# Fewer loads in the prologue, work in the lead-in, a side job on more slots, and a later normalization in an attention kernel on one Trainium2 core

## The chip, the cores and the metric

The kernel runs on one core of a Trainium2 chip. The core has TensorE (PE, matrix products; its weight loads are listed as PEld), VectorE (DVE), ScalarE (ACT), GpSimd (POOL) and SyncE (SP), whose queue issues all the transfers of this kernel. The metric is the device time of one execution in microseconds; a kernel's time is the median of several runs.

## The reference, cut to what matters

Two branches are computed on 2048 tokens of width 640 and mixed with a gate per token. Branch A is attention with 32 heads of 20 columns over four segments of 512 tokens, with a memory matrix per head that is read before and written after each segment. Branch B routes one token (the highest score) through a feed-forward layer and leaves all other tokens as they are.

```python
for s in range(N):                       # N = 4 segments of L = 512
    qs, ks, vs = q[:, :, s], k[:, :, s], v[:, :, s]
    p = softmax(einsum("bhqd,bhkd->bhqk", qs, ks) * scale + mask)
    a_dot = einsum("bhqk,bhkd->bhqd", p, vs)
    a_mem = einsum(phi(qs), M) / (einsum(phi(qs), z) + 1e-6)
    outs.append(g * a_mem + (1 - g) * a_dot)      # g: a gate per head
    M = M + einsum(phi(ks), vs); z = z + phi(ks).sum()
a = concat(outs) @ wo
...
idx = argsort(-(x @ w_r))[:1]            # the one routed token
y = (silu(x[idx] @ w_gate) * (x[idx] @ w_up)) @ w_down * sigmoid(r[idx])
b = x, with y added to row idx
return G * a + (1 - G) * b               # G = sigmoid((x * gate_w).sum(-1))
```

## The kernel before

The work is cut into 8 units (2 halves of the heads, 4 segments each) and 32 groups of 4 heads, four to a unit. Matrices are kept as a high and a low part, so each product of the projections is three matmuls.

**Projections.** For each unit nine jobs are computed in the order T0, T1, T2, V0, V1, T3, V2, T4, V3: a T job gives 128 columns of queries and keys for 512 tokens (15 matmuls of 512 columns), a V job gives the values of 128 tokens (15 matmuls of 320 columns, 322 in the first half, with two extra columns `rg` for the router and the gate). `load_t`, `load_v` and `load_x` bring raw weights and inputs into a ring of four buffers named `raw`; `split_t`, `split_v`, `split_x` make the two parts on ScalarE and VectorE or GpSimd (tiles `whi`, `wlo`, `xhi`, `xlo`). `prefetch(u, job)` says at which job each load and split is written. After a T job `evac_t` splits the result (`hi`, `lo`) and `place` writes it to DRAM (`stkq`, `stkk`); `bring_back` reads it from there as `qs` and `ks`, six matmuls into the next job, in the layout that the logits need. At that point the variable `groups[0]` also tells which groups have been placed. Small steps wait in a list `tail` and are taken at fixed points of the next job: `keys` (transposes `ktp`), `memory_read` (products `nm`), `memory_write` (products `mp`).

**Attention.** The main loop goes over groups n = -2 to 31, six slots each. `a_step` computes logits (`a`) of a group that comes later, from which VectorE takes row maxima (`junk`, `mx`); `m_split` and `m_rows` turn the maxima into two extra rows of `qs` (`mneg`, the transpose `mtp`, the copy `mr`, four small transfers `qs<-mr`), needed by `b_step` of that group at its slot 0. `b_step` computes the logits with the maxima subtracted (`bt`), ScalarE the exponentials (`p`), GpSimd the causal mask; `pv_step` multiplies with the values (`va`), in two halves, at slot 5 of the group and slot 1 of the next one. `norm` (transposes `otp`, then `rs`, `rs`, `ou` on VectorE) and `store` (`otok`) follow.

**What fills the time.** `fill(at)` runs projection matmuls until the projections are 3.7 groups ahead; it is called twice in each slot from group -1 on. In group -2 and before `a_step` the projections only run as far as `groups[0]` asks.

**The side job.** Routing and the feed-forward layer are a generator `ffn` whose steps end at each `yield 1`. It is started at slot 0 of group 13 and advanced by one step at each `pv_phase`, twice per group. `route` has 12 steps, each with a small transfer or a small operation: row maxima to DRAM (`rrow`), back as a row (`row`), its maximum (`top`), to DRAM (`sel`), back to all partitions (`all`), and this twice. `ffn_up` takes 10 steps (5 for the gate, 5 for the up matrix; each brings two weight tiles `wt` of 442 KB and multiplies those of the step before), `ffn_act` works on ScalarE, VectorE and GpSimd (`fe`) and goes through DRAM (`hrow`, `ht`), `ffn_down` takes 8 steps, and `yrow`, `yb`, `y` end it. At slot 0 of group 28 what is left of it is run at once (`f.finish()`), and then the last stage starts, `out_stage`: for each of 16 tiles of 128 tokens it loads `otok` (`ot`), transposes (`ttp`), splits (`oh`, `ol`), multiplies with `wo` (`acc` of line 721) and mixes.

**What sets the order.** TensorE and SP execute in the order in which the code is written. On the other engines a scheduler chooses a fixed order when the program is built. Small results of TensorE (`acc`, `ktp`, `nm`, `mp`, `mtp`, `otp`, `ffn`, `ttp`) share three PSUM buffers (`misc`).

Of the kernel before, what the change touches and what calls it, by code (L numbers as in the profile page):

```python
# [20 lines left out]
HH = H // NH  # L21
# [34 lines left out]
def tile_infini_mod(  # L56
# [100 lines left out]
    def w_tile(key):  # L157
        w, tag, bufs = (VC + 2, "wv", KT) if key[0] == "V" else (D, "w", KT + 1)
        hi = pool.tile([128, w], F32R, tag=tag + "hi", bufs=bufs, name="whi")
        lo = pool.tile([128, w], F32R, tag=tag + "lo", bufs=bufs, name="wlo")  # L160
        W[key] = hi, lo
        return hi, lo
# [21 lines left out]

    def load_w(key):
        if key[0] == "V":
            r = slice(128 * key[2], 128 * key[2] + 128)
            srcs = [columns("v", key[1], g, 2 * GC)[r] for g in (0, 2)]
            if key[1] == 0:
                srcs.append(wc[r, WQ:WQ + 2])  # L190
            raw_tile(key, *srcs)
        else:
            raw_tile(key, wo[128 * key[1]:128 * key[1] + 128, :])

    def split_w(key, eng=None):
        raw = raws.pop(key)
        hi, lo = w_tile(key)
        split(hi[:, :raw.shape[1]], lo[:, :raw.shape[1]], raw, eng or nc.gpsimd)
# [104 lines left out]
    def evac_v(u, c, acc):  # L303
        hf, s = divmod(u, SEG)
        nc.scalar.copy(sub(va[u % 2], c * (HH * VW + 11), [[VW, HH], [1, DH]]),
                       acc[:, :VC].rearrange("p (h d) -> p h d", d=DH))
        if hf == 0:
            nc.vector.tensor_copy(rg[:, :, 4 * s + c], acc[:, VC:VC + 2])
# [9 lines left out]
    def prefetch(u, job):  # L318

        hf, s = divmod(u, SEG)  # L320
        if u == 0:
            if job == "T0":
                load_t(0, 1)
                split_t(0, 1, nc.vector)
                load_t(0, 2)
            elif job == "T1":
                split_t(0, 2, nc.vector)
            elif job == "T2":
                split_v(0, (0, 1, 2, 3), nc.vector)
                load_v(0, (4,))  # L330
                load_t(0, 3)
            elif job == "V0":
                split_v(0, (4,), nc.vector)
                split_t(0, 3)
                load_t(0, 4)
            elif job == "V1":
                split_t(0, 4)
        if u == SEG:
            if job == "T0":
                load_v(1, (0, 1, 2, 3))  # L340
            elif job == "T1":
                split_v(1, (0, 1, 2, 3))
                load_v(1, (4,))
            elif job == "T2":
                split_v(1, (4,))
# [17 lines left out]

    def load_v(hf, ks_):
        for k in ks_:
            load_w(("V", hf, k))

    def split_v(hf, ks_, eng=None):
        for k in ks_:
# [501 lines left out]
```

## Time and profile before

| | |
|---|---|
| median of 3 runs | 762.35 us (755.8 to 767.57) |
| the profiled execution | 758.56 us |
| its span, first to last instruction | 756.6 us |
| TensorE busy | 662.8 us (88%) |
| VectorE, ScalarE, GpSimd busy | 428.1, 356.8, 213.9 us |
| granted TensorE clock, mean over the span | 0.935 of full speed |

The profiled execution lies 0.5% below the median. The span is shorter than the execution by 2.0 us, which lies around the instructions. A granted clock of 1.0 is 2.4 GHz, and one of 0.5 is 1.2 GHz.

### The profile page before, as it was taken

The page shows a single profiled execution, that of the slowest core. Times are in us where ns is not written, and L with a number is a line of the kernel's source. Part 1 is how long each engine was busy: PE and PEld are TensorE (multiplying, and loading weights), DVE is VectorE, ACT ScalarE, POOL GpSimd, SP SyncE. Part 2 cuts the span into 40 slices and gives each one's busy share as a digit, 9 for nine tenths or more (in the row PEclk, how much of TensorE's full clock was granted, in tenths as well). Part 3 has the DMA queues.
Part 4 walks back from the last instruction along what each step waited for, and adds up shares of the span by engine and source line. Part 5 has one row for each costly group of instructions (what it writes and reads, how often), then busy time and mean ns, then how long its engine had stood idle before and what let it go on. Part 6 is the DMA issues. An engine that isn't in the chain of part 4 may idle for free.

```text
span 756.6 us, 13400 instructions
## 1 busy us (share of the span) xinstructions
PE 662.8 (88%) x4496; PEld 448.6 (59%) x4496; DVE 428.1 (57%) x1498; ACT 356.8 (47%) x608; POOL 213.9 (28%) x322
## 2 busy tenths in 40 slices
PE   4278989998997999899979998999889656999997
PEld 2256656665664666456656665655566216777787
DVE  7235556665666467656645666666657314664453
ACT  5313546555566466555634555545545202444421
POOL 4102313332344355423411332234434100111100
PEclk9669999999999899999968999999999755999999
DMA  5726653646465557565852576768565634334453
GB/s 161 190 53 177 177 144 96 169 126 165 113 179 151 153 141 186 142 141 151 152 138 69 159 223 208 221 192 254 146 186 166 176 113 151 114 116 133 145 168 105
DMA packets 82932, 116.31 MB, mean 154 GB/s; under 512 B 37734, under 2 KB 43376, under 8 KB 82864
## 3 DMA queue, kind: packets, MB, share of 16 engines
q1 hardware_dynamic: 82864, 115.46, 55.8%
q8 instruction: 36, 0.59, 0.4%
q14 instruction: 32, 0.26, 0.1%
HBM read 72.94 MB, written 41.96 MB: 152 GB/s over the span
## 4 chain that ended last, share of the span: by engine, by line
PE 67%; DMA 13%; DVE 6%; ACT 6%; issue 5%; SPq 3%; POOL 0%; POOLq 0%; ACTq 0%
PE acc L391 17%; PE acc L396 9%; PE pv L497 9%; PE bt L477 9%; PE acc L721 7%; PE a L446 6%; PE nm L272 3%; DVE junk L449 2%; DMA wt<-in_wd_dram 2%; DMA wt<-in_wu_dram 2%; DVE lo L247 2%; DMA raw<-in_wc_dram 2%; PE ktp L263 2%; PE otp L518 1%; ACT hi L246 1%
## 5 line engine op out<-in xcount | busy, mean ns | idle before, releaser
L449 DVE CUSTOM_DVE_ANT_0 junk<-a,mask 128x512 bf16<-128x512 f32 (+3 forms) x512 | 249.9, 488 | 132.8 <-PE a L446 123.0
L481 ACT ACTIVATE p<-bt 128x768 f32<-128x768 f32 (+1 forms) x192 | 169.6, 883 | 198.3 <-PE bt L477 190.2
L484 POOL TENSOR_SCALAR_AFFINE_SELECT p<-p 128x256 f32<-128x256 f32 (+1 forms) x192 | 94.7, 493 | 350.1 <-ACT p L481 350.0
L446 PE MATMUL a<-ks,qs 60*128 60x256 f32 (+2 forms) x512 | 81.5, 349 | 26.3 <-DMA ks<-stkk 13.5
L477 PE MATMUL bt<-qs,ks 62*128 62x256 f32 (+2 forms) x512 | 95.8, 407 | 7.2 <-ACT p L481 5.0
L391 PE MATMUL acc<-xhi,whi 128*128 128x512 f32 x200 | 86.8, 434 | 10.0 <-ACT xhi L149 7.7
L391 PE MATMUL acc<-xhi,wlo 128*128 128x512 f32 x200 | 91.1, 456 | 0.0
L391 PE MATMUL acc<-xlo,whi 128*128 128x512 f32 x200 | 87.5, 438 | 0.0
L497 PE MATMUL pv<-p,va 128*32 128x512 f32 (+3 forms) x1024 | 84.9, 451 | 0.0
L477 PEld LDWEIGHTS bt<-qs,ks 62*128 62x128 f32 x512 | 44.5, 189 | 62.1 <-issue 40.7
L446 PEld LDWEIGHTS a<-ks,qs 60*128 60x128 f32 x512 | 48.6, 193 | 37.3 <-DMA ks<-stkk 13.8
L391 PEld LDWEIGHTS acc<-xhi,whi 128*128 128x128 f32 x200 | 39.8, 199 | 30.0 <-issue 12.3
L396 PE MATMUL acc<-wlo,xhi 128*128 128x322 f32 (+1 forms) x160 | 55.3, 345 | 0.0
L721 PE MATMUL acc<-whi,oh 128*128 128x320 f32 x160 | 53.2, 332 | 1.7 <-DVE ol L689 1.5
L396 PE MATMUL acc<-whi,xhi 128*128 128x322 f32 (+1 forms) x160 | 54.2, 339 | 0.0
L150 POOL TENSOR_TENSOR xlo<-raw,xhi 128x512 fp32r<-128x512 f32 x37 | 47.3, 1290 | 19.3 <-ACT xhi L149 18.1
L391 PEld LDWEIGHTS acc<-xlo,whi 128*128 128x128 f32 x200 | 39.8, 199 | 20.8 <-issue 14.7
L396 PE MATMUL acc<-whi,xlo 128*128 128x322 f32 (+1 forms) x160 | 51.6, 322 | 0.0
L721 PE MATMUL acc<-whi,ol 128*128 128x320 f32 x160 | 51.5, 322 | 0.0
L721 PE MATMUL acc<-wlo,oh 128*128 128x320 f32 x160 | 50.3, 314 | 0.0
L497 PEld LDWEIGHTS pv<-p,va 128*32 128x32 f32 x1024 | 27.3, 111 | 37.7 <-issue 27.8
L391 PEld LDWEIGHTS acc<-xhi,wlo 128*128 128x128 f32 x200 | 40.3, 202 | 13.6 <-issue 9.7
(105 smaller groups left out, 932.8 us busy)
## 6 DMA issues: line engine op xcount, KB each, us to landing
qs<-stkq SPq DMA_DIRECT2D x64, 240.0 KB
ks<-stkk SPq DMA_DIRECT2D x64, 240.0 KB
raw<-in_xT_dram SPq DMA_DIRECT2D x40, 256.0 KB
stkq<-hi SPq DMA_DIRECT2D x32, 320.0 KB
stkq<-lo SPq DMA_DIRECT2D x32, 160.0 KB
otok<-ou SPq DMA_DIRECT2D x32, 160.0 KB
xf<-in_x_dram SPq DMA_DIRECT2D x16, 320.0 KB
out_dram<-xf SPq DMA_DIRECT2D x16, 320.0 KB
```

The source lines that it names most:

```text
L150: eng.tensor_tensor(out=lo, in0=raw, in1=f32(hi), op=OP.subtract)
L247: nc.vector.tensor_tensor(out=lo[:, :L], in0=acc, in1=f32(hi)[:, :L], op=OP.subtract)
L272: nc.tensor.matmul(nm[:, c, :], e[:GC, 128 * c:128 * c + 128], mbd[:, g, :], start=True, stop=True)
L391: nc.tensor.matmul(acc, a, b, start=i == 0, stop=i == 3 * KT - 1)
L396: nc.tensor.matmul(acc[:, :w], a, b, start=i == 0, stop=i == 3 * KT - 1)
L446: nc.tensor.matmul(a[:, b, at:at + nw], q_, k_, start=True, stop=True)
L449: nc.vector.tensor_tensor_reduce(out=junk[:, :w], in0=a[:, b, at:at + w], in1=mask[:, L - w:], scale=1.0, scalar=-3e38, op0=OP.add, op1=OP ...
L477: nc.tensor.matmul(bt[:, b, at:at + nw], k_, q_, start=True, stop=True)
L481: nc.scalar.activation(pt, bt[:, :, at:at + w], AF.Exp, scale=SCALE)
L484: nc.gpsimd.affine_select(out=d, in_=d, pattern=[[0, 2], [0, k], [1, 128]], base=0, channel_multiplier=-1, compare_op=OP.is_ge, fill=0.0)
L497: nc.tensor.matmul(pv[n][32 * j:32 * j + 32, L - w:], va[u % 2][:, c, VW * h:VW * h + 32], pt_tiles[n, j % 2, min(c, 2)][:, j // 2, at:at ...
L721: nc.tensor.matmul(acc[:, :n], a_[:, 128 * k:128 * k + 128], b_[:, n * b:n * b + n], start=i == 0, stop=i == 3 * KT - 1)
```

## The change

The value weights of a half come in four loads (`VPARTS`: 3 or 2 blocks of 128 rows, two column ranges) instead of ten or fifteen, into one wide tile; in the first unit they are issued before the placed results of T0, or right behind them, and the loads for T3 and T4 later than before. Before the loop the projections run up to 1.9 groups, group -2 begins at slot 3, and `fill` runs in it too. `groups[0]` is set at the twelfth matmul of a job, not the sixth, and `tail` steps are taken after matmuls 6, 9, 12 and 14, not 4, 7, 10 and 13. Steps of the side job that brought weights end with `yield 2` and are still advanced by `pv_phase`; all others are advanced at the end of every slot. `norm` moves from slot 2 to slot 4 and `store` from slot 3 to slot 5. In `out_stage` a tile whose rows were not loaded ahead waits three half-slots after its loads.

```diff
+    VPARTS = ((0, 0, 3), (0, 3, 5), (1, 0, 3), (1, 3, 5))
+    def load_v(hf, i):
+        qt, k0, k1 = VPARTS[i]
+        w = 2 * GC + (2 if hf == 0 and qt == 0 else 0)
...
+        nc.sync.dma_start(t, columns("v", hf, 2 * qt, w).rearrange("(k p) m -> p k m", p=128)[:, k0:k1])
...
             if job == "T0":
                 load_t(0, 1)
+                load_t(0, 2)
+                load_v(0, 0)
                 split_t(0, 1, nc.vector)
-                load_t(0, 2)
             elif job == "T1":
+                load_v(0, 1)
+                load_v(0, 2)
                 split_t(0, 2, nc.vector)
+                load_v(0, 3)
             elif job == "T2":
-                split_v(0, (0, 1, 2, 3), nc.vector)
-                load_v(0, (4,))
+                for i in range(4):
+                    split_v(0, i, nc.vector)
+            elif job == "V0":
                 load_t(0, 3)
...
                         if i == 6:
                             bring_back()
+                        if i == 12:
                             groups[0] = landed
-                            if (u, job) == (0, "T1"):
-                                load_v(0, (0, 1, 2, 3))
...
-                        if i in (4, 7, 10, 13):
+                        if i in (6, 9, 12, 14):
...
             wt = [ffn_load(rows[t, :, 2 * FC * hf:2 * FC * hf + 2 * FC], 2 * FC, 128) for hf in range(2)]
-            yield 1
+            yield 2
...
-            loads(t)
+            if t not in ot and t not in rows:
+                loads(t)
+                for _ in range(3):
+                    yield None
...
         for f in side:
-            f.run(1.0)
-
+            if f.last == 2:
+                f.debt = 0.0
+                f.run(1.0)
+
+    proj.until(lambda: chunks[0] >= 1.9)
     for n in range(-2, NG):
-        for slot in range(6):
+        for slot in range(0 if n > -2 else 3, 6):
...
-            if n >= -1:
-                fill(6 * n + slot)
+            fill(6 * n + slot)
...
-            if n >= 1 and slot == 2:
+            if n >= 1 and slot == 4:
                 done = norm(n - 1)
-            if n >= 1 and slot == 3:
+            if n >= 1 and slot == 5:
                 store(n - 1, done)
                 ready[0] = n - 1
+            for f in side:
+                if f.last != 2:
+                    f.debt = 0.0
+                    f.run(1.0)
```

On SP's queue in the lead-in, between the placed results of T0 and the first keys (`ks_107`), the program before has this, behind the last of twelve value loads (the first row):

```order
L144 DMA raw<-in_wc_dram 128x2
L224 DMA stkq_72<-hi 80x2x512
L226 DMA stkq_72<-lo 80x512
L224 DMA stkk_76<-hi 32x2x512
L226 DMA stkk_76<-lo 32x512
L224 DMA stkk_77<-hi 16x2x512
L226 DMA stkk_77<-lo 16x512
L144 DMA raw<-in_wc_dram 128x160 x2
L144 DMA raw<-in_wc_dram 128x2
L168 DMA raw<-in_wc_dram 128x5x80 x2
L239 DMA qs_109<-stkq_72 60x1024 x2
L239 DMA ks_107<-stkk_76 60x1024 x2
```

The changed program has this at the same place, behind the first of its four value loads:

```order
L192 DMA raw<-in_wc_dram 128x2x162
L192 DMA raw<-in_wc_dram 128x3x160
L192 DMA raw<-in_wc_dram 128x2x160
L250 DMA qs_106<-stkq_71 60x1024 x2
L235 DMA stkq_72<-hi 80x2x512
L237 DMA stkq_72<-lo 80x512
L235 DMA stkk_76<-hi 32x2x512
L237 DMA stkk_76<-lo 32x512
L235 DMA stkk_77<-hi 16x2x512
L237 DMA stkk_77<-lo 16x512
L250 DMA qs_109<-stkq_72 60x1024 x2
L250 DMA ks_107<-stkk_76 60x1024 x2
```

The value loads no longer stand between T0's queries and T1's results, and the loads for T3 (`128x5x80 x2`) no longer stand ahead of the first keys.

On SP's queue at slots 2 and 3 of group 14 of the changed program, the second pass of the routing (`all`, `rrow`, `row`) and the rows of maxima for group 15 (`qs_106<-mr`) stand like this:

```order
L572 DMA sel<-top_3429 1x1
L250 DMA ks_113<-stkk_78 60x1024 x2
L575 DMA all_3505<-sel 128x1
L560 DMA rrow<-best 128x1
L474 DMA qs_106<-mr 1x8x128 x4
```

On VectorE of the changed program the source of that `rrow`, `best`, stands behind the reductions of the `a_step` of slot 5 of group 14 (the last two of them shown):

```order
L456 ISA junk,mx<-a,mask 128x128
L456 ISA mx 128x1
L556 SCALAR_TENSOR_TENSOR cand<-rg,all_3505,tok 128x16
L588 TENSOR_SCALAR sg<-sg 128x1
L558 TENSOR_REDUCE best<-cand 128x1
```

In the program before, the second `rrow` stood behind the maxima of its group and their store; now it stands ahead of them, and waits for a result that VectorE makes two slots after the place where it is written:

```order
L467 DMA qs_112<-mr 1x8x128 x4
L531 DMA otok<-ou 128x4x80
L553 DMA rrow<-best 128x1
L224 DMA stkq_71<-hi 80x2x512
L226 DMA stkq_71<-lo 80x512
```

On SP's queue at the end of the feed-forward layer, the program before had this at slot 0 of group 28:

```order
L595 DMA wt<-in_wd_dram 108x640 x8
L644 DMA yrow<-y 4x320
L649 DMA yb<-yrow 128x640
L649 DMA y_6637<-yrow 128x640
L239 DMA qs_109<-stkq_72 60x1024 x2
```

The changed program has the same end of the layer at slots 1 to 3 of group 24, with no run of weight loads ahead of it:

```order
L250 DMA ks_113<-stkk_78 60x1024 x2
L651 DMA yrow<-y 4x320
L144 DMA raw<-in_wo_dram 128x640
L656 DMA yb<-yrow 128x640
L656 DMA y_5849<-yrow 128x640
L474 DMA qs_106<-mr 1x8x128 x4
```

The eight weight loads in a row, the four last steps of `ffn_down`, are spread over slots of groups 21 to 23. Before `yrow`, the pair `hrow`, `ht` of `ffn_act` stands ahead of the rows of maxima that group 20 makes for group 21.

## Rows read from the trace of the kernel before

**Rows 1.** The page: shares of the span, then the granted clock in 40 slices.

```profile
PE 662.8 (88%) x4496; PEld 448.6 (59%) x4496; DVE 428.1 (57%) x1498; ACT 356.8 (47%) x608; POOL 213.9 (28%) x322
...
PEclk9669999999999899999968999999999755999999
```

**Rows 2.** Stretches: length; busy PE, PEld, DVE, ACT, POOL; clock, DMA share, GB/s.

```profile
24.00:37.75 13.75, 0.38 (x3) 0.01 (x1) 2.89 (x6) 4.94 (x11) 2.52 (x3) 0.63 0.79 193
...
73.40:357.50 284.10, 265.94 (x1879) 174.11 (x1876) 177.23 (x685) 161.93 (x275) 105.50 (x158) 0.99 0.57 149
...
403.40:593.10 189.70, 178.50 (x1308) 114.52 (x1308) 120.09 (x440) 98.03 (x165) 65.97 (x96) 0.98 0.66 188
...
596.90:632.30 35.40, 15.74 (x65) 5.47 (x65) 5.62 (x13) 2.98 (x5) 0.42 (x1) 0.56 0.56 168
...
632.30:642.00 9.70, 9.70 (x39) 8.30 (x39) 5.26 (x19) 3.29 (x7) 1.15 (x2) 0.51 0.09 30
```

**Rows 3.** Timeline of TensorE in the lead-in (start, length, line, tiles, idle before).

```profile
23.74 0.40 PE L391 MATMUL acc<-xlo,whi 128*128 128x512 f32 x1
...
23.98 0.40 PE L391 MATMUL acc<-xhi,whi 128*128 128x512 f32 x1
...
37.75 0.79 PE L446 MATMUL a<-ks,qs 60*128 60x512 f32 x1 [13.37 <-DMA ks<-stkk]
...
59.75 0.44 PE L446 MATMUL a<-ks,qs 60*128 60x384 f32 x2
```

**Rows 4.** Timeline of ScalarE in the lead-in.

```profile
22.36 0.59 ACT L246 CAST hi<-acc 128x512 fp32r<-128x512 f32 x1 [3.36 <-PE acc L391]
```

**Rows 5.** Timeline of SP's queue in the lead-in; the length is the issue.

```profile
19.95 5.61 SPq L144 DMA_DIRECT2D raw<-in_wc_dram  x12
...
25.66 0.38 SPq L224 DMA_DIRECT2D stkq<-hi  x1
...
32.40 0.85 SPq L239 DMA_DIRECT2D ks<-stkk  x2
```

**Rows 6.** Chain of waits, lead-in and the steady part (start, length, what).

```profile
32.84 5.73 DMA ks<-stkk
...
114.55 1.23 PE acc L396 x7
```

**Rows 7.** Timeline of GpSimd in the lead-in.

```profile
34.17 2.52 POOL L150 TENSOR_TENSOR wlo<-raw,whi 128x400 fp32r<-128x400 f32 x3 [20.82 <-ACT whi L149]
```

**Rows 8.** Chain of waits around group 28.

```profile
590.59 0.54 PE ffn L640 x8
...
596.92 4.52 DMA wt<-in_wd_dram
...
626.19 4.74 DMA ot<-otok
```

**Rows 9.** TensorE's longest waits over the whole span (total, times, longest).

```profile
PE mtp L462 <- DVE ou L523: 13.1, 6, 3.7
...
PE nm L272 <- DVE phi L254: 4.3, 4, 1.1
...
PE bt L477 <- DMA qs<-mr: 2.0, 2, 1.2
```

**Rows 10.** Timeline of VectorE around the normalization of group 8.

```profile
242.28 1.75 DVE L458 SCALAR_TENSOR_TENSOR mneg<-mx,mneg 128x16 fp32r<-128x16 f32 x1
```

**Rows 11.** Timeline of TensorE at the same place.

```profile
245.92 0.29 PE L462 MATMUL mtp<-identr,mneg 128*66 128x128 f32 x1 [3.21 <-DVE ou L523]
```

**Rows 12.** Timeline of SP's queue after the feed-forward layer.

```profile
618.43 0.55 SPq L644 DMA_DIRECT2D yrow<-y  x1
...
620.10 0.36 SPq L649 DMA_DIRECT2D yb<-yrow  x1
...
645.57 2.68 SPq L467 DMA_DIRECT2D qs<-mr  x4
```

**Rows 13.** The page: a costly group (busy us, mean ns of one | idle before).

```profile
L449 DVE CUSTOM_DVE_ANT_0 junk<-a,mask 128x512 bf16<-128x512 f32 (+3 forms) x512 | 249.9, 488 | 132.8 <-PE a L446 123.0
```

More of the change, by code (lines that the diff above doesn't have):

```diff
@@ L183, in split_t, with split_v @@
                     split(h_.bitcast(F32R), l_.bitcast(F32R), src, eng or nc.gpsimd)
-    def load_w(key):
[L186 to L193, printed above, removed]
+    VPARTS = ((0, 0, 3), (0, 3, 5), (1, 0, 3), (1, 3, 5))
+    def load_v(hf, i):
+        qt, k0, k1 = VPARTS[i]
+        w = 2 * GC + (2 if hf == 0 and qt == 0 else 0)
+        t = pool.tile([128, D], F32, tag="raw", bufs=4, name="raw")[:, :(k1 - k0) * w].rearrange("p (k m) -> p k m", m=w)
+        nc.sync.dma_start(t, columns("v", hf, 2 * qt, w).rearrange("(k p) m -> p k m", p=128)[:, k0:k1])
+        raws["V", hf, i] = t
+    def split_v(hf, i, eng=None):
+        raw = raws.pop(("V", hf, i))
+        qt, k0, k1 = VPARTS[i]
+        w = raw.shape[2]
+        hi, lo = W.get(("V", hf)) or w_tile(("V", hf))
+        c = slice(162 * qt, 162 * qt + w)
+        split(hi[:, k0:k1, c], lo[:, k0:k1, c], raw, eng or nc.gpsimd)
+    def load_w(key):
+        raw_tile(key, wo[128 * key[1]:128 * key[1] + 128, :])
     def split_w(key, eng=None):
@@ L197, in split_w @@
         hi, lo = w_tile(key)
-        split(hi[:, :raw.shape[1]], lo[:, :raw.shape[1]], raw, eng or nc.gpsimd)
+        split(hi, lo, raw, eng or nc.gpsimd)
     X = {}
@@ L323, in prefetch @@
                 load_t(0, 1)
+                load_t(0, 2)
+                load_v(0, 0)
                 split_t(0, 1, nc.vector)
-                load_t(0, 2)
             elif job == "T1":
+                load_v(0, 1)
+                load_v(0, 2)
                 split_t(0, 2, nc.vector)
+                load_v(0, 3)
             elif job == "T2":
-                split_v(0, (0, 1, 2, 3), nc.vector)
-                load_v(0, (4,))
+                for i in range(4):
+                    split_v(0, i, nc.vector)
+            elif job == "V0":
                 load_t(0, 3)
-            elif job == "V0":
-                split_v(0, (4,), nc.vector)
+            elif job == "V1":
                 split_t(0, 3)
                 load_t(0, 4)
-            elif job == "V1":
+            elif job == "T3":
                 split_t(0, 4)
@@ L339, in prefetch @@
             if job == "T0":
-                load_v(1, (0, 1, 2, 3))
+                for i in range(4):
+                    load_v(1, i)
             elif job == "T1":
[L342 to L345, printed above, removed]
+                for i in range(4):
+                    split_v(1, i)
         if s == SEG - 1 and hf + 1 < NH:
@@ L362, in prefetch @@
                 load_x(u + 1, k)
[L364 to L369, printed above, removed]
-            split_w(("V", hf, k), eng)
     def projections():
@@ L392, in projections @@
                         else:
-                            wh, wl = (t[:, :w] for t in W["V", hf, k])
+                            wh, wl = (t[:, k, :w] if hf == 0 else sub(t, (VC + 2) * k, [[162, 2], [1, 2 * GC]])
+                                      for t in W["V", hf])
                             h_, l_ = xh[:, 128 * j:128 * j + 128], xl[:, 128 * j:128 * j + 128]
@@ L636, in ffn_down @@
             wt = [ffn_load(rows[t + i], D, 108) for i in range(2)]
-            yield 1
+            yield 2
             ps = psum.tile([128, 512], F32, tag="misc", bufs=3, name="ffn")
@@ L740, in __init__ @@
         def __init__(self, gen):
-            self.gen, self.live, self.debt = gen, True, 0.0
+            self.gen, self.live, self.debt, self.last = gen, True, 0.0, None
         def run(self, ns):
@@ L746, in run @@
                 try:
-                    cost = next(self.gen)
+                    cost = self.last = next(self.gen)
                 except StopIteration:
```

16 lines of the change are left out of this document (8 added, 8 removed).

## The prediction

> **What bounds the kernel now.** I read the page first. TensorE is busy for 88% of the span, so it is the engine to follow, and its granted clock stands at full speed in most of the 40 slices; the digits fall at slices 2 and 3 (the lead-in), a little at 14, at 21 and 22, and at 32 to 34 [rows 1]. Then I cut the span at the lead-in and at the last of these [rows 2]. From group 0 to group 16, 73.4 to 357.5 us, TensorE is busy for 265.9 of 284.1 us at a clock of 0.99: nothing can be gained there but single waits. In 24.0 to 37.75 it is busy for 0.4 of 13.75 us, and in 596.9 to 632.3 for 15.7 of 35.4 us at a clock of 0.56. Those two holes and the short waits between them are what the change can reach. The list of waits says what the short ones are: the transposes `mtp` waited 13.1 us in all for `ou`, six times, and the products `nm` 4.3 us for `phi` [rows 9]. A slot lasts 284.1 / 16 / 6 = 2.96 us [rows 2]; I use that below. All sums are made against the profiled execution, 758.56 us (span 756.6), which lies 0.5% below the median of 762.35, and the result is raised by that at the end.
>
> **Part A, the prologue.** Before, group 0's first logits start at 37.75 us after a wait of 13.37 us for the keys [rows 3]. Why so late: T1's result was being split from 22.36 us on [rows 4], but SP was issuing twelve value loads from 19.95 to 25.56 us, so the first piece of T1 went out at 25.66 us, and between the last piece and the keys stood five more loads; the keys were issued at 32.40 us [rows 5] and took 5.73 us to land [rows 6]. One issue costs 5.61 / 12 = 0.47 us. After the change three value loads stand ahead of T1 (1.4 us, done by the time the split ends near 23 us) and none behind: 2.7 us are won ahead and 5 x 0.47 = 2.3 us behind, so the keys are issued at 27.4 and land at 33.6 us, if they take as long. Meanwhile TensorE has work: nine matmuls of T2 at 0.24 us (the starts at 23.74 and 23.98 us [rows 3]) to 26.4 us, then a pause of about 1.5 us for the value splits, which stand behind T2's result on ScalarE and VectorE, and V0, 15 x 0.18 = 2.6 us (1.23 us for 7 [rows 6]), to 30.5 us. So some 3 us of the 13.4 are left. V1 then takes it to about 37 us. T3 needs its weights: GpSimd's part of their split ran from 34.17 to 36.69 us [rows 7], and SP now comes to these loads behind T2's four pieces, 0.5 to 2 us later, so 37.5 to 38.5 us. T3 with two steps of logits between lasts 4.5 us at full clock and 8 us at half. At 59.75 us the program before had done exactly this much (the logits of that row follow T3 [rows 3]); the changed one is there at 42 to 46 us. I take a gain of 16 us. Ends: 10 if the transfers, at 193 GB/s and 0.79 of their engines' time in the hole [rows 2], bring T3's weights 6 us later; 19 if TensorE is never below full clock.
>
> Against merging speaks a rule of the Trainium skill (Perfetto Trace Analysis, DMA Optimizations): splitting DMAs lets some of the work start sooner. By it V0 starts one merged load later, an estimate of 249 KB in place of 80 KB at 193 GB/s [rows 2], 0.9 us, and A would be 15.
>
> **Part B, the end of the side job.** It has 37 steps, and two a group from slot 1 of group 13 make 30 by group 28. The seven left were run at once: four pairs of weight loads from 596.92 us on, each followed by its matmuls, and the row through DRAM. From 596.9 to 632.3 us, 35.4 us, TensorE's matmuls are those four steps, 4 x 0.54 = 2.2 us at full clock [rows 8], and about 2.8 us of other work; the next 9.7 us ran at a clock of 0.51 [rows 2], which is 4.8 us lost. Of 35.4 + 4.8 the 2.2 and 2.8 us stay: 35 us. With the change 13 short steps take 13 slots, the loads 18 more half-groups, the rest a few slots, so the job ends at slot 3 of group 24 and nothing is left at group 28. The first rows of `out_stage` still have to come, 4.74 us [rows 8], now with three half-slots (4.4 us) of other work to cover them; I leave 2 us for that. B is 33 us, ends 28 (that load waits in full, and the clock falls once more) and 36. The moved steps cost nothing new: 18 steps with weights stay at two a group, only some ten groups earlier, and in groups 18 to 27, where 14 of them ran, TensorE was busy for 178.5 of 189.7 us [rows 2], the same 94% as without them.
>
> **Part C, the normalization and the small steps.** At group 9 `mtp` started at 245.92 us after 3.21 us of waiting [rows 11]; its own input `mneg` was done at 242.28 + 1.75 = 244.03 us [rows 10], and the rest was `ou`, whose PSUM buffer it had to take over. With `norm` two slots later that part, 1.9 of 3.2 us, goes: of 13.1 us 7.7. The steps after matmul 6 give `phi` two matmuls (0.5 us) more, and others between them: 2.5 of 4.3 us [rows 9]. The clock digits of slices 14, 21 and 22 (8, 6 and 8 [rows 1]), behind such waits, stand for 10 to 18 us at half clock, so 9.5 to 15 us lost at most; I take 3 us, since the rows don't say that all of it follows these waits. For new waits, `otp` in a busier slot, I subtract 2. C is 11 us, ends 3 and 24. The later `store` matters to `out_stage` alone, two slots.
>
> **Part D, what gets slower.** A faster side job puts its transfers closer together on SP, and SP waits in order. Two places. At group 14 the second `rrow` stands ahead of the maxima rows of group 15 and waits for `best`, which VectorE makes behind the four reductions of slot 5, 4 x 0.49 = 1.95 us [rows 13] and 0.5 us of its own. Then follow `rrow`'s issue, 0.55 us as `yrow`'s, four issues of 2.68 us, and a landing of 620.10 - 618.98 = 1.12 us [rows 12]: 6.8 us, where `b_step` of group 15 is due after 2.96. TensorE waits 3.9 us, and everything on SP behind it too. At group 20 `hrow` and `ht` stand ahead of the rows of group 21 and wait for two GpSimd products behind a mask and a split; by 2.52 / 3 = 0.84 us for 400 columns [rows 7] these are done some 4.5 us into slot 3, and 1.67 + 0.5 + 3.8 us later the rows are there: 10.5 us, due after 8.9, so 1.6 us. With a fall of the clock behind each I take 8 us lost; ends 0 (the scheduler's order hides them) and 14.
>
> A second rule of the skill (DMA: Bandwidth & Descriptors, Anatomy of one DMA) gives a fixed cost of about 2 us for each DMA. The row above has 1.67 us for `yrow`; by the page each of the four trips in D is 0.3 us longer, D 9, the sum 1 us more.
>
> **The sum.** 758.6 - 16 - 33 - 11 + 8 = 706.6 us; times 762.35 / 758.56 that is 710 us. The ends of the four parts, taken together as independent, and runs that lie 6 us apart give 695 to 726 for this case.
>
> **Rivals.** *The transfers set the lead-in.* If A is only 5 us, because the same bytes must go through first, and D is at its end of 14, the time is 710 + 11 + 6 = 727 us. For it: the DMA share of 0.79 in the hole. Against: that hole is 13 us long, with SP's order as its cause. *All half-clock stretches go.* With C at 24 and B at 36 the time is 710 - 13 - 3 = 694 us. For it: the clock fell behind waits only; against: such stretches follow waits for transfers too, as both holes show, and those are not all removed. *The hole stays.* If the first `out_stage` loads or the side job's last row still hold TensorE at group 28 for 30 us, the time is 740 us. *Slower: weights ahead of the maxima rows.* The 18 pairs of weight tiles, 885 KB each, go through the same queues as `qs<-mr`. If at groups 15 to 24 each pair held `b_step` for its 4.5 us (a load of 4.52 us [rows 8]), that is 81 us, and the time is 790; it decides from (777 - 710) / 18 = 3.7 us a pair on. Against: `b_step` waited for those rows twice in the whole span, 2.0 us in all [rows 9], with the same loads at the same slots.
>
> **How the numbers follow.** The sum's case has 0.66, the lead-in 0.14, the clock 0.14, the hole 0.03, the slower one 0.03. The range of 690 to 730 takes in the first three. A measurement tells about 2% from no change here, 15 us: 747 and 777 are the bounds. Faster 0.93 (the first three less 0.01), same 0.04, slower 0.03.
>
> **What would show it.** A: no wait of over 5 us for `ks` before group 0, and the first exponentials near 57 us instead of 73. B: no stretch at half clock when `out_stage` begins, and `yrow` at group 24. C: `mtp` no longer waits for `ou`. D: a wait of `bt` for `qs<-mr` at groups 15 and 21. Wrong would make it: a clock of 0.5 over tens of us after group 13, or waits for weights inside groups 15 to 24.

## The result, and the profile after

The changed kernel takes 733.58 us (median of 4 runs, 723.78 to 734.49) beside 762.4 us before: a ratio of 0.9616, 95% interval 0.9517 to 0.9715. In more rounds of the same kernel it was 0.9602 (0.9562 to 0.9643). So it is faster by some 29 us, where 52 were forecast, and the time lies above the range. The profiled execution took 723.78 us (span 721.9), 34.8 us less than the one of before. It was the quickest of its four, so the profiles show some 6 us more gain than the medians do.

The page after has TensorE's busy tenths and its granted clock in 40 slices (compare [rows 1]):

```profile
PE   4888999999999999884999997989989996999997
...
PEclk9779999999999999997999997899999997999999
```

Of the low places of before, those at slices 14, 21 and 22 are gone, the lead-in is less deep, and the stretch of three slices near the end has become one. Two are new, at slices 19 and 25 to 26 (near 330 and 450 us). The windows below show the lead-in, groups 0 to 12, and groups 14, 20 and 28 (columns as in [rows 2]):

```profile
33.00:62.50 29.50, 24.17 (x98) 15.67 (x97) 13.82 (x55) 8.04 (x18) 6.24 (x6) 0.83 0.56 157
62.50:292.80 230.30, 218.34 (x1559) 144.21 (x1557) 151.44 (x568) 135.46 (x229) 89.90 (x133) 0.99 0.57 151
...
311.40:337.60 26.20, 16.10 (x117) 11.08 (x116) 9.70 (x42) 7.96 (x15) 3.74 (x7) 0.85 0.41 102
...
435.70:462.00 26.30, 23.75 (x136) 15.66 (x135) 17.30 (x48) 11.89 (x21) 9.57 (x12) 0.74 0.42 121
...
589.30:619.00 29.70, 23.14 (x148) 17.06 (x146) 15.06 (x50) 11.28 (x20) 4.46 (x8) 0.83 0.51 144
```

Group 14 takes 26.2 us with 16.1 of them busy, group 20 runs at a clock of 0.74, group 28 at 0.83. TensorE's longest waits, to be held against [rows 9] (total, times, longest):

```profile
PE bt L484 <- DMA qs<-mr: 17.4, 7, 10.1
PE a L453 <- DVE mx L456: 12.1, 14, 2.6
...
PE ttp L692 <- DMA ot<-otok: 5.8, 1, 5.8
```

The waits of `mtp` for `ou` are gone; in their place stand 17.4 us for the maxima rows, 10.1 us of them in one wait.

To see where each kernel loses time I cut its span at the first exponentials of each group and took from each stretch the matmuls started in it, each at the pitch of its form at full clock (0.23 us for 512 columns of a projection, 0.147 for 322, and so on, as they follow each other in rows with a clock of 1.0). These sum to 604.3 us for the kernel before and for the changed one; what is over is lost, to waits and to half clock (a granted clock of 0.5). The table has this loss in the profiled execution of each kernel, in us by groups, and the ratio of its times to the kernel before:

| kernel | ratio | lead-in | groups 0-12 | 13-16 | 17-19 | 20-21 | 22-27 | 28 | 29-end |
|---|---|---|---|---|---|---|---|---|---|
| before | 1 | 45.6 | 28.2 | 7.3 | 14.8 | 2.0 | 8.2 | 35.8 | 10.4 |
| changed | 0.9616 | 34.7 | 23.8 | 19.7 | 3.3 | 7.8 | 7.9 | 11.3 | 9.1 |
| changed, more rounds | 0.9602 | 34.3 | 25.3 | 23.6 | 2.9 | 6.4 | 10.6 | 11.5 | 9.6 |
| A alone | 0.9857 | 35.3 | 37.3 | 10.3 | 10.9 | 1.6 | 12.7 | 35.9 | 11.5 |
| B alone | 0.9854 | 44.9 | 37.0 | 19.9 | 3.3 | 8.6 | 11.3 | 10.3 | 8.6 |
| C alone | 0.9876 | 45.9 | 28.8 | 7.5 | 7.2 | 0.4 | 9.8 | 35.7 | 10.6 |
| without B | 0.9725 | 35.1 | 28.5 | 11.0 | 8.7 | 0.4 | 8.4 | 32.8 | 11.7 |
| without C | 0.9776 | 35.2 | 31.0 | 23.6 | 2.5 | 10.2 | 13.1 | 10.5 | 8.1 |
| one packet | 0.957 | 32.4 | 25.3 | 15.0 | 6.1 | 7.3 | 7.7 | 11.7 | 9.8 |
| second `rrow` later | 0.9565 | 35.1 | 27.1 | 24.6 | 2.8 | 6.3 | 9.2 | 10.3 | 9.7 |
| one packet, 1 slot later | 0.9583 | 34.9 | 24.0 | 18.8 | 4.9 | 8.1 | 7.7 | 11.7 | 9.1 |
| one packet, 3 slots later | 0.948 | 35.3 | 23.7 | 9.0 | 4.8 | 7.6 | 10.3 | 11.4 | 9.2 |
| reciprocal in 4 | 0.9627 | 33.8 | 25.7 | 23.0 | 3.9 | 5.7 | 10.9 | 10.8 | 9.4 |
| earlier load | 0.9578 | 30.6 | 31.5 | 23.2 | 3.2 | 6.3 | 10.6 | 4.7 | 10.6 |
| the last three | 0.9509 | 34.2 | 28.6 | 10.8 | 4.9 | 5.9 | 16.4 | 6.8 | 9.6 |
| the same without pieces | 0.9373 | 34.2 | 28.6 | 9.7 | 2.8 | 7.8 | 9.4 | 6.1 | 9.3 |
| the same with 3 pieces | 0.9453 | 33.6 | 28.3 | 10.2 | 5.0 | 14.5 | 6.3 | 6.1 | 10.5 |

The second and third rows are two executions of one kernel. They differ by up to 3.9 us in a column, so smaller differences between two rows tell nothing. The profiled execution of A alone was a slow one (761.46 us, the median of its runs 750.5), so only its lead-in is read.

So the lead-in gave 10.9 us and group 28 gave 24.5, but groups 13 to 16 took 12.4 back and groups 20 and 21 another 5.8. Groups 17 to 19 gave 11.5: in the kernel before, group 17 alone lost 11.2 us, at a wait of `mtp` for `ou` of 3.69 us and the half clock behind it. What kept `ou` was VectorE, which stood at the routing's maximum `top` for the row that the second `rrow` had written:

```profile
386.82 0.27 DVE L559 TENSOR_REDUCE top<-row 1x1 f32<-1x128 f32 x1 [2.67 <-DMA row<-rrow]
```

B, which moves the routing, and C, which moves `norm`, each take this loss away (3.3 and 7.2 us in that column).

### The profile page after: what moved, and what is told of

The parts are those of the page before. It is cut to its first block, busy times and chain, and to the rows that moved or that the text cites. A ratio compares the mean times of both kernels' runs of the same rounds, so it can differ in the third digit from the quotient of the medians.

```text
span 721.9 us, 13325 instructions
## 1 busy us (share of the span) xinstructions
PE 650.9 (90%) x4496; PEld 446.7 (62%) x4496; DVE 440.7 (61%) x1497; ACT 357.4 (50%) x606; POOL 214.0 (30%) x321
## 4 chain that ended last, share of the span: by engine, by line
PE 71%; DMA 8%; ACT 8%; DVE 6%; issue 4%; SPq 2%; POOL 1%; ACTq 0%; DVEq 0%; POOLq 0%
PE acc L398 17%; PE acc L731 11%; PE bt L484 9%; PE pv L504 9%; PE acc L404 8%; PE a L453 6%; DMA qs<-mr 4%; PE nm L283 3%; DVE junk L456 3%; PE otp L525 2%; PE mp L300 2%; ACT phi L263 2%; ACT hi L257 1%; PE ktp L274 1%; DVE lo L258 1%
## 5 line engine op out<-in xcount | busy, mean ns | idle before, releaser
L484 PE MATMUL bt<-qs,ks 62*128 62x256 f32 (+2 forms) x512 | 96.5, 404 | 25.1 <-DMA qs<-mr 17.4
L398 PE MATMUL acc<-xhi,whi 128*128 128x512 f32 x200 | 90.3, 451 | 11.7 <-ACT xhi L149 7.8
L398 PE MATMUL acc<-xlo,whi 128*128 128x512 f32 x200 | 89.0, 445 | 0.2 <-POOL xlo L150 0.2
L398 PE MATMUL acc<-xhi,wlo 128*128 128x512 f32 x200 | 87.4, 437 | 0.5 <-POOL wlo L150 0.5
L504 PE MATMUL pv<-p,va 128*32 128x512 f32 (+3 forms) x1024 | 82.2, 439 | 0.0
L453 PEld LDWEIGHTS a<-ks,qs 60*128 60x128 f32 x512 | 48.0, 190 | 28.4 <-DVE mx L456 10.6
L398 PEld LDWEIGHTS acc<-xhi,wlo 128*128 128x128 f32 x200 | 40.2, 201 | 17.4 <-issue 12.1
```

The costliest lines, as they stand in the source:

```text
L398: nc.tensor.matmul(acc, a, b, start=i == 0, stop=i == 3 * KT - 1)
L453: nc.tensor.matmul(a[:, b, at:at + nw], q_, k_, start=True, stop=True)
L484: nc.tensor.matmul(bt[:, b, at:at + nw], k_, q_, start=True, stop=True)
L504: nc.tensor.matmul(pv[n][32 * j:32 * j + 32, L - w:], va[u % 2][:, c, VW * h:VW * h + 32], pt_tiles[n, j % 2, min(c, 2)][:, j // 2, at:at ...
```

## The experiments

### The parts alone

A alone is the new prologue on the kernel before, B alone the side job and the start of `out_stage`, and C alone the later places of the small steps, of `norm` and of `store`. Each part is several edits, and no run takes a part's edits from one another.

> The kernel before with part A alone: merged value loads in the order of need, projection during the lead-in; side job, small steps, normalization and out_stage as before. By the prediction's term A: 16 us, first exponentials near 57 us, 758.6 - 16 = 743, ratio 0.979. By what the trace of the changed kernel shows (T3 runs at half clock and with five steps of logits between, exponentials at 62.5 us, not 73.4): 11 us, ratio 0.986, and nothing of it is lost later. Rival: the 11 us are given back behind the lead-in, because the exchange of transfers is then the limit: ratio over 0.993.

> The kernel before with part B alone: side job on more slots and the three half-slots between out_stage's first loads and their use. By the prediction's terms: B 33 less D 8, so 25 us, ratio 0.967. By the trace of the changed kernel: the first ot load still holds TensorE for some 5.8 us at group 28 and the clock then falls for one stretch of 10 us, so B is 24 to 26 us; the wait for qs<-mr at group 15 behind rrow costs 10 us, but the program before lost as much behind its second rrow at group 17 (11 us), so about 25 us again, ratio 0.967. Both theories give one time here; they differ in where: 5 to 6 us for ot at group 28 and one half-clock stretch, against 2 us and none, and a wait of about 10 us against 3.9 us for qs<-mr at group 15.

> The kernel before with part C alone: norm two slots later, store two slots later, the small steps after matmuls 6, 9, 12, 14. By the prediction: 11 us (5.7 us of it waits of mtp for ou, 2.5 of nm for phi, 3 of clock, less 2), ratio 0.985. By the comparison of the two traces group by group (groups 2, 6, 10 gain 9 us, the others lose 0.5 us each): 4 us, ratio 0.994. Rival: nothing, because the small steps' new places make as many waits as they take away: ratio 1.0 and mtp's waits under 2 us all the same.

A gave 0.9857 (0.9795 to 0.9918), 10.9 us; B 0.9854 (0.9646 to 1.0061), 11.1 us, uncertain; C 0.9876 (0.9832 to 0.992), 9.4 us. The three sum to 31.4 us and the whole gives 29 to 30, so by their medians they add up, though B's interval leaves this open and B and C share the loss at group 17. C is near its term of 11, A a third under its 16. B alone shows both faults at once: group 28 falls from 35.8 to 10.3 us as in the whole, and groups 13 to 16 rise from 7.3 to 19.9.

In C alone `mtp` no longer waits for `ou`, but other waits of about 1 us each, 2.7 at most, stand in its place (8.1 and 5.0 us in all before):

```profile
PE a L446 <- DVE mx L449: 14.5, 17, 1.8
...
PE bt L477 <- ACT p L481: 11.3, 12, 2.7
```

### The parts taken away

From the changed kernel, B or C was put back to its state of before.

> The changed kernel without part B: side job and out_stage's start as before. The prediction has 25 us for B less D: the time would be 734 + 25 = 759, ratio 0.996. The trace has 24.5 us at group 28 and 2 behind it, less 11 at groups 13 to 17 and 20: about 15 us, 749 us, ratio 0.982. The run of B alone gave 11 us with an interval too wide to tell.

> The changed kernel without part C: norm, store and the small steps at their places of before. The prediction has 11 us for C; the run of C alone gave 9.4 us (0.9876). If these waits are as many with A and B in place, the time is 743 us, ratio 0.974. If B and C overlap (norm's new slot is also that of the steps with weights), C is worth under 5 us here, ratio under 0.967.

Without B the ratio is 0.9725 (0.9643 to 0.9807): against 0.9602, B less D is worth 9 us, not 25. Without C it is 0.9776 (0.9694 to 0.9857): C is worth 13 us in place, a little over its term. By the table B takes 21.3 us from group 28 (32.8 to 11.5), and 8 us from groups 17 to 19 and the end together, and gives back 12.6 in groups 13 to 16, 6.0 in 20 and 21 and 2.2 in 22 to 27. That leaves 8.4 us, close to the times; another 4.0 us of the two profiles lie in the lead-in and groups 0 to 12, where the two programs are alike.

### Groups 13 to 16: who holds the maxima rows

In the changed kernel, VectorE first (start, duration, line, operation), then SP, then TensorE:

```profile
325.30 0.23 DVE L556 SCALAR_TENSOR_TENSOR cand<-rg,all,tok 128x16 f32<-128x16 f32 x1
...
325.57 0.17 DVE L558 TENSOR_REDUCE best<-cand 128x1 f32<-128x16 f32 x1
...
325.76 0.35 SPq L560 DMA_DIRECT2D rrow<-best  x1
326.21 2.76 SPq L474 DMA_DIRECT2D qs<-mr  x4
...
336.37 1.16 PE L484 MATMUL bt<-qs,ks 62*128 62x512 f32 x2 [10.10 <-DMA qs<-mr]
```

Up to the issue this is what the prediction has: `best` behind VectorE's reductions, `rrow` on SP behind `best`, the four rows behind `rrow`. Issued at 326.21 and 2.76 us long, they should land by 326.21 + 2.76 + 1.12 = 330.1, and TensorE, ready at 326.3, should wait 3.8 us. It waited 10.1. The completions of the rows' transfers came between 332.8 and 336.6 us, though the last packet of the rows started at 329.7; ahead of them in the queues stood `rrow`, 128 packets of 4 bytes to DRAM. By the Trainium skill (DMA: Bandwidth & Descriptors, Queues, rings and completion order) a transfer's semaphore step lands only after every earlier write of its DMA engine; the completions here agree. By the Trainium skill (DMA: Bandwidth & Descriptors, Specifications) a write of under 512 bytes is a read, a change and a write; no run here shows that by itself. The first test replaces these packets by one of 512 bytes, at the same place:

```diff
-            nc.sync.dma_start(rrow[k].rearrange("(p o) -> p o", o=1), best[:, k:k + 1])
+            tp = psum.tile([128, 128], F32, tag="misc", bufs=3, name="rtp")
+            nc.tensor.transpose(tp[:1, :], best[:, k:k + 1], identf)
+            row = one.tile([1, 128], F32, name=f"row{k}")
+            nc.vector.tensor_copy(row, tp[:1, :])
+            nc.sync.dma_start(rrow[k:k + 1], row)
```

> The changed kernel, where the row of 128 maxima goes to DRAM as one packet of 512 bytes from one partition (TensorE transposes best, VectorE copies it), in place of 128 packets of 4 bytes, at the same place in SP's order and behind the same wait. Theory one (the 4-byte packets: their completions came up to 10 us after the issue, and those of qs<-mr behind them at 332.8 to 336.6 us though the data had moved by 329.7): the wait of bt at group 15 falls from 10.1 to about 4 us, the stretch of half clock behind it goes, the groups 13 to 15 lose 11 instead of 20 us, and the time falls by 9 us, to 0.95 of the kernel before. Theory two (SP's order alone, the wait for best): the wait stays at 10 us and the time as it is, 0.962.

The long wait of `bt` is gone, but TensorE, in order too, now waits for `best` itself, which VectorE makes only when `all` has landed (the profile names `sg`, an operation of VectorE next to `best`):

```profile
PE rtp L561 <- DVE sg L592: 4.8, 1, 4.8
PE bt L484 <- DMA qs<-mr: 3.9, 4, 1.6
```

Groups 13 to 16 lose 15.0 us instead of 19.7; the ratio of 0.957 (0.9402 to 0.9739) can't be told from the changed kernel's. The first pass of the routing shows the packets by themselves, since nothing waits for `best` there and the order is the same. `rrow` stands right ahead of the rows of group 14, and `bt` waits for these rows in the changed kernel (the first line), but not with one packet (the second):

```profile
310.43 0.82 PE L484 MATMUL bt<-qs,ks 62*128 62x512 f32 x2 [2.42 <-DMA qs<-mr]
```

```profile
310.53 0.49 PE L484 MATMUL bt<-qs,ks 62*128 62x512 f32 x2 [0.97 <-ACT p L488]
```

The second test leaves the 4-byte packets and lets the second `rrow` come a slot later, behind the rows of group 15:

```diff
             yield 1
+            if k == 1:
+                yield 1
             nc.sync.dma_start(rrow[k].rearrange("(p o) -> p o", o=1), best[:, k:k + 1])
```

> The changed kernel with the second rrow one slot later, so that it stands behind the maxima rows of group 15 on SP and no longer holds them for best. The packets stay 128 of 4 bytes. If SP's order is all there is to it, the wait of bt for qs<-mr at group 15 (10.1 us) goes and the time falls by 9 us, ratio 0.95. If the completion of the 4-byte packets is half of it (as the run with one packet suggests, where the waits for qs<-mr fell from 17.4 to 3.9 us in all and TensorE itself waited 4.8 us for best), the transfers that stand behind rrow now, the two loads of x, are held for some 8 us instead; TensorE needs them a group later, so the wait is short and the gain still 6 to 9 us. Rival: the held loads cost as much at group 16 as the rows did at group 15, and the time stays.

The time stays, as the rival of that text has it, but not for the reason it gives (the held loads, at group 16): the rows are free, and the loss moves to group 15 (15.3 us of the 24.6), where VectorE now takes the wait. In this run, SP, VectorE and TensorE:

```profile
333.88 0.33 SPq L562 DMA_DIRECT2D rrow<-best  x1
341.49 0.25 SPq L565 DMA_DIRECT2D row<-rrow  x1
...
345.08 0.28 DVE L568 TENSOR_REDUCE top<-row 1x1 f32<-1x128 f32 x1 [6.38 <-DMA row<-rrow]
...
347.70 0.80 PE L453 MATMUL a<-ks,qs 60*128 60x512 f32 x2 [6.31 <-issue]
```

`row`'s load waits for the end of `rrow`, 7.6 us after its issue; VectorE stands 6.38 us at `top`, with the reductions of the next logits behind it; TensorE then waits for these reductions, done at 347.6 us ("issue" names only that the profile found no releaser). With one packet the same step is short. In the run with the single packet three slots later:

```profile
327.83 0.25 SPq L568 DMA_DIRECT2D rrow<-row  x1
328.92 0.23 SPq L570 DMA_DIRECT2D row<-rrow  x1
```

That is 1.1 us instead of 7.6; with the second transpose one slot later it is 2.5 us. The next two runs have the one packet and the second transpose one slot and three slots later (`yield 1` once or three times more for `k == 1`).

> The changed kernel with both: one packet of 512 bytes made by a transpose, and the second one a slot later, so that neither TensorE nor SP waits for best. If the two causes together make the 20 us that groups 13 to 15 lose over their matmuls, these lose under 9 us, as the groups around them (2 to 3 each), and the time falls by 11 us, ratio 0.946. If SP's order was not the cause, the loss moves to groups 15 and 16 and the time stays at 0.96.

> The changed kernel with the row of 128 maxima as one packet of 512 bytes, made by a transpose, and the second transpose three slots later, so that neither SP nor TensorE waits for best and no packets of 4 bytes are written. If the two causes found so far (SP and TensorE, both in order, behind best; the completions of 4-byte packets) are all there is to groups 13 to 16, their loss of 19.7 us falls to 8 (the kernel before, without its second rrow, lost 7.3 there), and the time by 10 to 12 us, ratio 0.947. If something else holds these groups, they lose 15 us or more again and the ratio stays near 0.96.

One slot is too early: `best` comes behind the landing of `all`, TensorE still waits 2.49 us for it, and half clock follows (18.8 us lost, 0.9583, 0.9517 to 0.9649). With three slots groups 13 to 16 lose 9.0 us, and the time is 717.51 us, a ratio of 0.948 (0.942 to 0.954), 9 us under the changed kernel. So two things made this loss together, the engines that stand in order behind `best` and the slow end of the 4-byte packets; where only one is taken away, another wait takes its place. No run has the 4-byte packets three slots later, and none tells the number of the packets from their size.

### Group 20: the reciprocal

In the changed kernel, VectorE, TensorE, and a window of the stretch behind:

```profile
443.00 2.85 DVE L628 RECIPROCAL fe<-fe 128x432 f32<-128x432 f32 x1
```

```profile
446.95 0.80 PE L453 MATMUL a<-ks,qs 60*128 60x512 f32 x2 [2.55 <-DVE mx L456]
```

```profile
446.00:456.20 10.20, 9.25 (x33) 6.89 (x34) 5.25 (x19) 1.82 (x4) 4.70 (x5) 0.50 0.12 28
```

TensorE waits 2.55 us for maxima that VectorE makes behind the reciprocal, and 10.2 us at half clock lie around its end, with TensorE busy for 9.25 of them, some 4.6 us lost. `bt` waits for no rows at group 21. The edit takes the reciprocal in four pieces.

```diff
-        nc.vector.tensor_scalar(e, e, 1.0, None, op0=OP.add)
-        nc.vector.reciprocal(e, e)
+        for c in range(0, FC, FC // 4):
+            yield 1
+            nc.vector.tensor_scalar(e[:, c:c + FC // 4], e[:, c:c + FC // 4], 1.0, None, op0=OP.add)
+            nc.vector.reciprocal(e[:, c:c + FC // 4], e[:, c:c + FC // 4])
```

> The changed kernel with the reciprocal of the feed-forward's gate, 2.85 us in one piece on VectorE at 443.0 us, in four pieces a slot apart. Prediction's term D put the loss of group 20 on SP's order (hrow and ht ahead of the maxima rows). If it is VectorE instead (logits waited 2.55 us for mx behind the reciprocal, then 10.2 us at half clock), the 7.5 us that group 20 loses fall to about 2, and the time by 5 us, ratio 0.955. If it is SP's order, group 20 or 21 still loses 7 us, with a wait of bt for qs<-mr.

Group 20 loses 3.9 us instead of 7.5 and no wait for the rows at group 21 appears, which speaks against SP's order. But a wait of 2.13 us for maxima stays, since three of the four pieces still stand among the same reductions on VectorE (446.43 to 449.6 us), and the ratio, 0.9627 (0.9563 to 0.9691), shows no gain. In more rounds of the changed kernel, with the reciprocal whole, a wait of 2.91 us at this place had only 3.4 us at half clock behind it. So that the reciprocal makes the wait is read from VectorE's order; this run doesn't show it.

### Group 28: the first load of the last stage

In the changed kernel, SP, then TensorE, then a window:

```profile
594.60 0.77 SPq L250 DMA_DIRECT2D qs<-stkq  x2
...
596.31 0.86 SPq L517 DMA_DIRECT2D ot<-otok  x2
```

```profile
601.48 1.33 PE L692 MATMUL ttp<-identf,ot 128*128 128x128 f32 x5 [5.80 <-DMA ot<-otok]
```

```profile
599.60:609.80 10.20, 7.86 (x28) 6.25 (x28) 4.34 (x9) 3.26 (x6) 0.42 (x1) 0.50 0.39 129
```

The edit writes the start of `out_stage` one slot earlier and lets two half-slots more pass before the first use; TensorE's order stays, and on SP the loads of `ot` and `xf` stand ahead of `qs<-stkq` (some operations of VectorE and ScalarE at group 28 change places).

```diff
-            if n == 28 and slot == 0:
+            if n == 27 and slot == 5:
-                for _ in range(3):
+                for _ in range(5):
```

> The changed kernel with out_stage's first load two places earlier on SP, ahead of the loads of queries and keys at group 28, its use on TensorE at the same place. If the wait of 5.8 us for ot is set by when SP comes to that load (596.3 us, behind the queries' load, which waits for the pieces), it is issued 3 us earlier, the wait falls to under 3 us and the half-clock stretch of 10 us at 599.6 us goes: 6 to 8 us less, ratio 0.953. If the load is slow for another reason (its landing of 5 us), the wait stays at 5 us and the clock falls as before: no change.

The wait falls to 1.11 us, the stretch at half clock goes, and group 28 loses 4.7 us instead of 11.3:

```profile
605.01 0.76 PE L692 MATMUL ttp<-identf,ot 128*128 128x128 f32 x5 [1.11 <-DMA ot<-otok]
```

The ratio is 0.9578 (0.9521 to 0.9635). By itself it can't be told from 0.9602. In this profile groups 2 and 6 lost 6 us more; the last section comes back to that.

### All together

> The changed kernel with the row as one packet three slots later, the reciprocal in four pieces and out_stage's first load earlier on SP. If the three losses are separate, their gains add: about 11 at groups 13 to 16, 6.6 at group 28 and 2 to 4 at group 20, so 20 us, ratio 0.935. If they share a cause (the clock falls anyway, somewhere else), the sum is under 10 us, ratio 0.95 or more.

> The changed kernel with the row as one packet three slots later and out_stage's first load earlier on SP, the reciprocal in one piece. If the loss of 12 us at group 22 in the run with all three came from the four pieces (they shift the weight steps so that the load of wd is waited for, 5.8 us), it is 1 to 2 us here, and the gains of 11 and 6.6 us add: ratio 0.939. If the fall of the clock at groups 2 and 6 (3 us each, in that run and in some others with the same orders there) belongs to the earlier load, it stands here too, and the ratio is 0.947.

> As the run before, with the reciprocal in three pieces, so that the weight steps stand as many slots after a half-product step as in the changed kernel (six slots later in all, not seven). If the place of the weight steps against the half-product steps made the wait of 5.8 us for wd, it is gone, group 20 loses under 1 us and group 22 1 to 2: ratio 0.937. If a later side job itself makes it, group 22 loses over 8 us again: ratio 0.95.

> The changed kernel as it is, in more rounds. Its profiled execution took 723.8 us, the three others 733 to 734. If the clock's falls at groups 2, 6 and behind them differ from execution to execution with the same order, the times spread over 722 to 735 and the half-clock time in the profile differs by 10 us or more from 59 us; the ratio is 0.955 to 0.965. If the first execution was the odd one, all lie at 733 to 735.

The three cures together gave 720.0 us, 0.9509 (0.9446 to 0.9572), no better than the row's alone: the reciprocal in pieces shifts the weight steps, and TensorE waits for weights of `ffn_down`. In the run with four pieces, at group 22 (SP issued the load at 480.23 us, when TensorE had been ready since 478.64):

```profile
PE ffn L656 <- DMA wt<-in_wd_dram: 6.2, 2, 5.8
```

With three pieces the wait stands at group 21, although the steps keep their place against the half-product steps, so the forecast that the wait would go is wrong:

```profile
PE ffn L656 <- DMA wt<-in_wd_dram: 6.6, 1, 6.6
```

Why SP comes late to that load stays open. Without the pieces there is no such wait, and the time is 711.52 us (709.02 to 718.16), a ratio of 0.9373 (0.9324 to 0.9423): the fastest kernel of this study, 18 us under the changed one by times of the same chip (729.04 for that). The changed kernel in more rounds spread over 728.12 to 731.81 us, which is neither of the two forecasts (722 to 735, or all at 733 to 735); its profile has 6.6 us more of span than the first one, 3.9 of them in groups 13 to 16.

## Why the prediction was wrong

The parts and their signs were right, and so were the places of D's first wait and of B's gain; the sizes failed. Most of it is B less D, 25 us in the sum and 8 to 11 measured, and the step there is D's "a landing of 620.10 - 618.98 = 1.12 us" for `rrow`, whose end came 7.6 to 10.2 us after its issue. A is 5 us short.

**A, 16 us forecast, 10.9 measured** (its low end was 10). The order was as predicted: keys issued at 28.40 us, not 27.4, no wait of 13 us for them, T3 started at 39.16, not 37.5 to 38.5. The mis-sized step is "T3 with two steps of logits between lasts 4.5 us at full clock and 8 us at half".

```profile
34.03 0.47 PE L453 MATMUL a<-ks,qs 60*128 60x512 f32 x1 [0.35 <-DMA ks<-stkk]
...
39.16 0.50 PE L398 MATMUL acc<-xhi,whi 128*128 128x512 f32 x1 [1.64 <-ACT whi L149]
39.59 0.53 PE L453 MATMUL a<-ks,qs 60*128 60x384 f32 x2
...
43.08 0.80 PE L453 MATMUL a<-ks,qs 60*128 60x256 f32 x4
...
45.82 0.79 PE L453 MATMUL a<-ks,qs 60*128 60x512 f32 x2
...
48.97 0.69 PE L453 MATMUL a<-ks,qs 60*128 60x384 f32 x2
```

Three steps of logits stand between, and from 39.8 us on all of it ran at half clock, behind waits of 1.64 and 0.53 us: 9.8 us from the first matmul of T3 to the logits behind it. So the state that I had put at 42 to 46 us came at 49.0, 59.75 before, and the first exponentials at 62.5 instead of 57.

**B, 33 us forecast, 24.5 at group 28.** The seven steps vanished, `yrow` went out at 526.5 us, in group 24, as said, and the weight steps at groups 15 to 24 cost nothing of note: `ffn` waited 1.1 us for weights in the whole span. What failed is "I leave 2 us" for the first load of `out_stage`, and "no stretch at half clock when `out_stage` begins". The working lets three half-slots of other work cover the load from its issue on. But SP issued the load only at 596.31 us, behind the loads of queries and keys, and TensorE had done that work by 595.7. So it waited 5.8 us, and of the 10.2 us at half clock it was busy for 7.9, which cost another 3.9. With the earlier load both went.

**C, 11 us forecast, 9.4 alone and 13 in place.** Right in size, and only in part for the reasons given. The waits named went, but others came in their place, and what counts is the half clock behind either. In the profile of C alone groups 0 to 12 lose as much as before (28.8 and 28.2 us): groups 1, 5 and 9, where `mtp` had waited up to 3.2 us, lose less, and groups 2 and 6 lose more. Its gain stands at groups 17 to 19 (14.8 to 7.2 us). The term's "10 to 18 us at half clock" does not fit its own "9.5 to 15 us lost", since half clock costs half of its length; this touches the upper end of C alone.

**D, 8 us forecast (its high end was 14).** Against the kernel without B it is 12.6 + 6.0 us. The wait for `best` ahead of the maxima rows was as predicted, 3.8 us of the 3.9; but the price of the transfer itself was missed, since I took `rrow` to be a small one like `yrow`. The fixed 2 us for each transfer that the prediction quotes would have missed it too. So the 3.9 us that TensorE was to wait became 10.1, with half clock for 3.8 us behind them. For the same reason a place counts that D does not have: the first `rrow`, ahead of the rows of group 14 (2.42 us). D's second place, `hrow` ahead of the rows, cost nothing; there TensorE waited 2.55 us for maxima behind VectorE's reciprocal. Nor has the sum the 5.8 us that B gives at groups 17 to 19.

**The remainder.** The forecast was made against the profiled execution and raised by 0.5%. The profiled execution of after lies 1.3% under its own median, which adds 6 us to the miss. Of the rivals the first comes nearest with 727 us, but through its D of 14 and not its A of 5. None has the price of `rrow`, and no pair of weights held the maxima rows (`ffn` waited 1.1 us for weights). With the late rows and the late first load cured, the kernel has a ratio of 0.9373, 714.6 us where the forecast had 710. That these are so near is partly luck: the cures also take away most of the 8 us that D had as lost, and A stays 5 us short.

## What to carry to other kernels

When a background job is moved to an earlier place, price each of its small transfers by its packets, not its bytes, and ask at the new place which engine stands in order behind it: VectorE, TensorE and SP can each take over the same wait. Take a wait away at its source and place, both, before judging a cure, and remember that a wait of a few us can cost as much again, or nearly, when the clock falls behind it (5.8 and 3.9 us at group 28). The cost of a stage's first load is set by what stands ahead of it on the queue, so put that load ahead of transfers that themselves wait.

## What the runs showed that I had not expected

A transfer of 512 bytes in 128 packets of 4 bytes to DRAM took 7.6 us and more until the load that waits for it could be issued, one of a single packet 1.1 to 2.5 us. What was queued behind the former completed late although its data had moved (data by 329.7 us, completions from 332.8 us on).

The clock's fall is not fixed by the program. At group 22 the changed kernel waits 0.97 and 0.66 us in its first profile, and 0.98 and 0.65 us in the one of more rounds. Then it runs on at full clock in the first (the first line) and at half clock in the second:

```profile
486.40:493.20 6.80, 6.80 (x57) 5.42 (x45) 4.32 (x19) 3.98 (x8) 1.46 (x3) 1.00 0.59 167
```

```profile
489.70:496.50 6.80, 6.80 (x36) 5.23 (x29) 2.27 (x9) 2.26 (x4) 0.92 (x2) 0.50 0.56 175
```

The kernel with the earlier load is like the changed one up to group 27, and the two differ in the same way. At group 2 the changed kernel has two waits, of 0.98 and 0.66 us, and so has the one with the earlier load, at the same place and of the same length (0.98 and 0.66 us):

```profile
101.01 0.49 PE L484 MATMUL bt<-qs,ks 62*128 62x512 f32 x2 [0.98 <-ACT p L488]
102.17 0.44 PE L453 MATMUL a<-ks,qs 60*128 60x384 f32 x2 [0.66 <-DVE mx L456]
```

Then the one runs on at full clock and the other at half for 6.8 us; the windows behind these waits:

```profile
101.00:107.80 6.80, 6.13 (x53) 4.83 (x53) 4.46 (x21) 3.77 (x8) 2.00 (x4) 1.00 0.69 208
```

```profile
99.40:106.20 6.80, 6.80 (x39) 5.21 (x39) 1.89 (x8) 1.99 (x5) 1.15 (x2) 0.50 0.43 116
```

The Trainium skill (TensorE: Matmul & The Clock Gate, Part 1) calls the number of slow matmuls at a kernel's start run-variable; here the same holds in the middle of one. It costs some 3 us a time, at groups 2, 6 and 22, so a single profile, as the one the forecast was scaled by, can stand above or below the median. That executions of one kernel lie up to 10 us apart may come of it in part; no run here shows how much.
